# Loading the second MLP's weights earlier and with more room to land, and the keys of the first eight groups once

## The chip, the cores and the metric

One core of a Trainium2 chip runs the whole program. The metric is the time of one execution on the device in microseconds (us), and the figure quoted is the median of three executions. TensorE (PE) does the matrix products, VectorE (DVE), ScalarE (ACT) and GpSimd (POOL) the elementwise work, and SyncE (SP) issues nearly all DMA transfers. Each engine, and SP's queue of transfers too, runs its instructions in the order in which the program lists them: an instruction that waits holds up all that stand behind it on its engine.

## The reference

Three stages, each feeding the next, in float32 to the user (the weights arrive as float64):

```python
# q, k, v: 4 batches x 8 heads x 576 positions x 64
scores = scale * q @ k^T, masked to 0 <= row - column < 64
x = softmax(scores) @ v                  # 2304 tokens x 512
h = x @ w_in                             # 512 -> 2048
x = (h * sigmoid(1.702 * h)) @ w_out     # 2048 -> 512
xn = x / sqrt(mean(x * x) + 1e-6) * rms_g
out = (silu(xn @ w_gate) * (xn @ w_val)) @ w_out2   # 512 -> 1536 -> 512
```

## The kernel before

**Tiles.** The 2304 tokens are 36 attention groups of 64 tokens (nine per batch); each group attends to two neighbouring blocks of 64 keys. The first MLP takes the tokens in six blocks of 512, 256, 384, 384, 384 and 384. A block is 16 steps, one for each 128 of the 2048 hidden columns: an up product, the gate, and a down product two or more steps later. So there are 96 steps: 0 to 15 are the block of 512 ("block one"), 16 to 31 the block of 256 ("block two"), and from 32 on four blocks of 384. The second MLP follows in 36 units.

**Order.** No engine order is written by hand. Each operation is given to a planner (`Planner`, `pl.op`) with a cost for each engine that may run it, a priority `prio` (mostly the number of the step in which it is due; a smaller one goes first), what it reads and writes, and the tile buffers that it opens. `emit` plays the operations through in time: whenever an engine is free it takes, of those whose inputs are there and whose buffer is free, the one of least priority. What comes out is only an order for each engine and for SP's queue. A transfer counts there as done 2.2 us after its cost (bytes / 320 GB/s), and `late` adds to that: readers are put so much further down the order. On the chip the true waits are kept by semaphores. The tiles of a kind are taken in turn, and a tile is free when its last user is done.

**Second MLP's weights, first pass.** While the first MLP runs, the 36 weight pieces of the second are prepared (`b_narrow`, from line 1151): for each of 12 column chunks a gate, a value and an output piece. `w_narrow` (line 331) loads a piece of 512 KB into a tile of kind `raw` (line 336), and turns its float64 bits into float32: one ACT operation (line 340) and three of DVE (lines 344, 348, 354). The first MLP's 32 pieces went through the same three `raw` tiles in block one, the last of them loaded at 120.8 us. Two gate pieces (or two value pieces) make a pair: four sums and differences on DVE or POOL (line 1172) fill in their free halves, both tiles are stored to DRAM (`wp`, line 1175), and only when a store has landed is its `raw` tile free for another piece. Output pieces leave their `raw` tile for one of kind `y` and are stored from there (line 1158). Piece i has the place p = n0 + i * (n1 - n0) / 36 among the steps, with n0 = 34 and n1 = 76; it may be loaded once step int(p) - 2 has been run on PE, and its load has priority p, the work on it p + 3. Only output pieces have `late`, of 5 us. The first of these loads is issued at 194.8 us, the last at 423.8 us.

**Scatter at a block's end.** `a_finish` (from line 640) stores the block's result and the root mean squares: 1.5 KB go from a tile into DRAM one word at a time (`rs<-ss`, line 700), on SP's queue as well.

**Attention.** A group's chain is: scores on PE (line 428, in the first eight groups 432 and 435), mask and maximum on DVE, powers on ACT, normalization on POOL, transposition (on PE, or from group 18 on with DVE's 32 x 32 transpose, line 520, and copies of blocks by ACT and POOL, lines 312 and 314), values on PE (line 487). Keys, queries and values come in by lines 405, 398 and 413. The first eight groups run ahead of all else, from 4.5 to 31 us, with tiles of their own (`q0`, `k0`, `v0`): neighbouring groups share a block of keys, which each loads again.

Of the kernel before, what the change touches and what calls it, by code (L numbers as in the profile page):

```python
# [9 lines left out]
F32 = mybir.dt.float32  # L10
F32R = mybir.dt.float32r
I32 = mybir.dt.int32
# [5 lines left out]
P = 128  # L18
W = 64
# [182 lines left out]
def dma(nbytes):  # L202
    return max(nbytes / 320e3, 0.45)
# [3 lines left out]
def window_attention_two_moe_kernel(ctx: ExitStack, tc: tile.TileContext, ins, out):  # L207
    nc = tc.nc
    qh, kh, vh, w_in, w_out, w_gate, w_val, w_o2, rms_g = ins
    NBAT, NBLK = qh.shape[0], qh.shape[1]  # L210
    NT, DM = out.shape
    NK = DM // P
# [10 lines left out]
    NBA = len(sizes)  # L223
# [5 lines left out]
    NS = ngrp[0]  # L229
# [18 lines left out]
    ident = const.tile([P, P], F32, name="ident")  # L248
# [7 lines left out]
    start = sctx.enter_context(tc.tile_pool(name="start", bufs=1))  # L256
# [22 lines left out]
        "e": (at, 1, [P, NK, P], F32),  # L279
        "pt": (at, 1, [P, NK, P], F32),  # L280
        "t1": (at, 1, [P, NK, P], F32),
        "q0": (start, 4, [P, NK, 2 * W], F32),
        "k0": (start, 3, [P, 2, NK, W], F32),
        "v0": (start, 3, [P, DM], F32),
        "e0": (start, 4, [P, NK, P], F32),
        "pt0": (start, 1, [P, NK, P], F32),
# [9 lines left out]
    def make(b):  # L296
        if b.kind == "pt":
            b.tile = pts
            return pts
        if b.kind == "xa":  # L300
            turn = xa_turn[0] = 1 - xa_turn[0]
            b.tile = words(SUMS)[:, turn * 512:(turn + 1) * 512].rearrange("p (k c) -> p k c", k=NK)
            return b.tile
        p, n, shape, dt = KINDS[b.kind]
        b.tile = p.tile(shape, b.dt or dt, tag=b.kind, name=b.kind, bufs=n)
        return b.tile
# [19 lines left out]
    START = "start pool"  # L326
# [1 line left out]

    w32 = {}

    def w_narrow(key, src, prio, after=(), apart=False):
        rb = Buf("raw")
        fb = Buf("y") if apart else rb

        def fetch(e):
            nc.sync.dma_start(out=make(rb), in_=src.bitcast(I32).rearrange("p (n two) -> p n two", two=2))

        def scaled(e):
            high = rb.tile[:, :, 1].bitcast(F32)
            nc.scalar.activation(out=high, in_=high, func=AF.Copy, scale=2.0 ** -112)  # L340

        def shifted(e):
            low = rb.tile[:, :, 0]
            nc.vector.tensor_scalar(out=low, in0=low, scalar1=29, scalar2=None, op0=ALU.logical_shift_right)

        def joined(e):
            low, high = rb.tile[:, :, 0], rb.tile[:, :, 1]
            nc.vector.scalar_tensor_tensor(  # L348
                out=low, in0=high, scalar=3, in1=low, op0=ALU.logical_shift_left, op1=ALU.bitwise_or)

        def signed(e):
            low, high = rb.tile[:, :, 0], rb.tile[:, :, 1]
            to = make(fb).bitcast(I32) if apart else high
            nc.vector.scalar_tensor_tensor(
                out=to, in0=high, scalar=-2147483648, in1=low, op0=ALU.bitwise_and, op1=ALU.bitwise_or)

        got = pl.op({"D": dma(P * 4096)}, fetch, prio - 3, new=[rb], after=after, late=5.0 if apart else 0.0)
        pl.op({"A": act(512)}, scaled, prio, w=[rb])
        pl.op({"V": dve(512, True)}, shifted, prio, w=[(rb, "low")], after=[got], port="V")
        pl.op({"V": dve(512)}, joined, prio, w=[rb], r=[(rb, "low")], port="V")  # L360
        if apart:
            pl.op({"V": dve(512)}, signed, prio, r=[rb, "at"], new=[fb], port="V")
        else:
            pl.op({"V": dve(512)}, signed, prio, r=["at"], w=[rb], port="V")
        w32[key] = fb
# [25 lines left out]
    def wkey(g):  # L391
        b, i = divmod(g, NBLK)
        return b, max(i - 1, 0)
# [6 lines left out]
    def load_k(g, prio, kind="k"):  # L400
        if wkey(g) in kw:
            return
        b, i = wkey(g)
        t = kw[b, i] = Buf(kind)
        pl.op({"D": dma(P * 2048)}, lambda e: nc.sync.dma_start(out=make(t), in_=kh[b, :, i:i + 2]), prio, new=[t])

    def load_v(g, prio, kind="v"):
        if wkey(g) in vw:
            return
        b, i = wkey(g)  # L410
        t = vw[b, i] = Buf(kind)
        pl.op({"D": dma(P * 2048)},
              lambda e: nc.sync.dma_start(out=make(t), in_=vh[b, i * W:(i + 2) * W]), prio, new=[t])
# [4 lines left out]

    def attention(g, p0, step, ekind="e", ptkind="pt", norm=("G",), ptev=("A", "V"), hi=("A",)):
        q, k, v = q_of.pop(g), kw[wkey(g)], vw[wkey(g)]  # L420
        sb, eb, nb, ub, rb = Buf(f"y{g % 3}" if g < NS else "abank"), Buf(ekind), Buf("nm"), Buf("su"), Buf("rc")
        tb, pb, ob = Buf("bank" if g < NS else "abank"), Buf(ptkind), Buf("abank")
        extra = [START] if ekind == "e0" or ptkind == "pt0" or q.kind == "q0" or k.kind == "k0" or v.kind == "v0" else []

        def scores(e):
            s = make(sb)
            for p in range(NK):
                nc.tensor.matmul(s[:, p * P:(p + 1) * P], q.tile[:, p], k.tile[:, :, p], start=True, stop=True)  # L428

        def masked_scores(e):  # L430
            s = make(sb)
            nc.tensor.matmul(s.rearrange("p (k c) -> p k c", k=NK), ident_r,
                             (n_first if g % NBLK == 0 else n_rest).to_broadcast([P, NK, P]), start=True, stop=False)
            for p in range(NK):
                nc.tensor.matmul(s[:, p * P:(p + 1) * P], q.tile[:, p], k.tile[:, :, p], start=False,
                                 stop=(p == NK - 1))

        def highest_of(e):
# [59 lines left out]
        c = (g * W) % RING // W  # L498
        d = step
        if g < NS:  # L500
            pl.op({"T": 1.09}, masked_scores, p0, r=[q, k, "mask", "negative", "ident", *extra],
                  w=[("xh", c), ("xl", c), "scores order"], new=[sb])
            pl.op({"V": dve(512) + 0.1}, highest_of, p0, r=[sb], new=[nb])
            pl.op({"A": 4 * act(128, True, 2)}, powers_of, p0, r=[sb, nb, *extra], new=[ub, eb])
        else:
            pl.op({"T": 0.872}, scores, p0, r=[q, k, *extra], w=[("xh", c), ("xl", c), "scores order"], new=[sb, eb],
                  after=vals[NS - 1:NS] if g >= NS else ())
            pl.op({"V": dve(512)}, masked, p0, r=[sb, "mask"], w=[eb])
            pl.op({"V": dve(512)}, highest, p0, r=[eb], new=[nb])
            pl.op({"A": 4 * act(128, True, 2)}, powers, p0, r=[nb], w=[eb], new=[ub])  # L510
# [234 lines left out]
    def both(n, alone=False):  # L745
        return {"V": dve(n)} if alone else {"G": pool(n), "V": dve(n)}
# [336 lines left out]
    for g in range(NS):  # L1083
        late = g >= 2
        load_q(g, -90 + 2 * g, "q0" if late else "q")
        load_k(g, -89 + 2 * g, "k0" if g > 2 else "k")
        load_v(g, -84 + 2 * g, "v0" if g > 2 else "v")
    for g in range(NS):
        attention(g, -60 + g, 0.5, "e0" if g >= 2 else ("e", "t1")[g], "pt0" if g % 2 else "pt",
# [48 lines left out]
        b_list.append((("v", c), w_val[c], c - c % 2 + 1))  # L1138
        b_list.append((("o", c), w_o2[c], c + 2))
    b_list.sort(key=lambda x: x[2])  # L1140
    n0, n1 = first[2] + 2, first[NBA - 1] - 4

    def ex_open(e):
        actx.close()
# [6 lines left out]
    def b_narrow(i):  # L1151
        (kind, c), src, _ = b_list[i]
        p = n0 + i * (n1 - n0) / len(b_list)
        key = ("w32d", "o", c) if kind == "o" else ("w32d", c - c % 2 + "gv".index(kind), c % 2)
        w_narrow(key, src, p + 3, after=[ups[int(p) - 2]], apart=kind == "o")
        b = w32.pop(key)
        if kind == "o":
            pl.op({"D": dma(P * 2048)}, lambda e: nc.sync.dma_start(out=w32o_d[c], in_=b.tile), p + 3, r=[b], w=[key])
            return
        n = key[1]  # L1160
        if c % 2 == 0:
            halfway[n] = b
            return
        pair = (halfway.pop(n), b)

        def word(h, k, lane):
            return pair[h].tile[:, k * 256:(k + 1) * 256, lane].bitcast(F32)

        for to, x, y, op in (((0, 0), (1, 0, 1), (1, 1, 1), ALU.add), ((0, 1), (0, 0, 0), (0, 0, 1), ALU.subtract),
                             ((1, 0), (0, 0, 1), (1, 0, 1), ALU.subtract), ((1, 1), (0, 1, 1), (0, 1, 0), ALU.subtract)):  # L1170
            xs = [(n, "sum", *v[:2]) for v in (x, y) if v[2] == 0]
            fn = lambda e, to=to, x=x, y=y, op=op: eng[e].tensor_tensor(out=word(*to, 0), in0=word(*x), in1=word(*y), op=op)
            pl.op(both(256), fn, p + 3, r=[*pair, *xs], w=[(n, "sum", *to)], port="GV")
        for h in range(2):
            pl.op({"D": dma(P * 4096)}, lambda e, h=h: nc.sync.dma_start(
                out=w32p_d[n][:, h].bitcast(I32), in_=pair[h].tile), p + 3,
                r=[pair[h], (n, "sum", h, 0), (n, "sum", h, 1)], w=[("w32d", n, h)])

    plans.sort()
# [97 lines left out]
```

## Time and profile before

| | us |
|---|---|
| median of three runs | 937.48 (937.11 to 937.95) |
| the profiled execution, whole | 937.76 |
| its span, first to last instruction | 936.0 |
| PE busy | 909.0 |
| DVE busy | 648.8 |
| ACT busy | 436.4 |
| POOL busy | 275.3 |

| stretch of the span, us | what PE does there |
|---|---|
| 4.5 to 33 | scores, transposes and values of the first eight groups |
| 33 to 128 | block one (512 tokens), with four groups |
| 128 to 193 | block two (256 tokens), with six groups |
| 193 to 504 | blocks three to six, with 18 groups |
| after | the second MLP |

The profile lists each engine's instructions with start and length, and for an engine that stood idle what ended its wait. A time such as "us, times, longest" adds up such waits. PEclk is the share of full clock that TensorE was granted; it has two levels, 1.0 (2.4 GHz) and 0.5 (1.2 GHz), and a value between them is a mean over the stretch.

### The profile page before, as it was taken

The numbers are of one execution on the slowest core, as the hardware profiler recorded it, in microseconds if no ns is written. First come the engines' busy times: TensorE is split into PE (matmuls) and PEld (weight loads), VectorE is DVE, ScalarE is ACT, GpSimd is POOL, SyncE is SP. The second block draws the span as 40 slices with busy tenths as digits, with TensorE's granted clock in tenths as the row PEclk, the third lists the DMA queues.
The fourth block names the chain that finished last, engine by engine and source line by source line (L and its number), as shares of the span: only waits on it lengthen the run. The fifth ranks groups of instructions, "written<-read, shape, count | busy, mean of one in ns | idle before, by whom it ended". The sixth has DMA issues, their size and how long they took to land.

```text
span 936.0 us, 15370 instructions
## 1 busy us (share of the span) xinstructions
PE 909.0 (97%) x5436; PEld 843.1 (90%) x5436; DVE 648.8 (69%) x1237; ACT 436.4 (47%) x1078; POOL 275.3 (29%) x389
## 2 busy tenths in 40 slices
PE   8899999998999999999999999999999999999998
PEld 7787789988899999989999889998999999999997
DVE  5999974465777677675367888878767556555553
ACT  6666664464566567456336534454322224322222
POOL 4111021132345345333012633334223225222210
PEclk9899999999899999999999999999999999999999
DMA  8756532348666566753565999977987677976651
GB/s 274 237 182 203 175 121 56 109 139 192 224 220 205 180 228 240 184 205 122 68 236 172 302 280 332 369 277 246 319 247 209 204 204 235 291 204 205 203 153 67
DMA packets 86536, 194.63 MB, mean 208 GB/s; under 512 B 12726, under 2 KB 36027, under 8 KB 84924
## 3 DMA queue, kind: packets, MB, share of 16 engines
q1 hardware_dynamic: 66108, 137.02, 45.4%
q0 software_dynamic: 20352, 56.63, 20.5%
q8 instruction: 43, 0.70, 0.3%
q14 instruction: 33, 0.27, 0.1%
HBM read 140.13 MB, written 53.50 MB: 207 GB/s over the span
## 4 chain that ended last, share of the span: by engine, by line
PE 69%; DVE 13%; DMA 9%; issue 3%; ACT 3%; POOL 1%; SPq 1%; DVEq 0%; ACTq 0%; POOLq 0%
PE bank L912 8%; PE bank L913 8%; PE bank L914 8%; PE y L628 4%; PE y L630 4%; PE y L629 4%; PE bank L555 4%; PE bank L554 4%; PE bank L556 4%; PE y L1013 3%; PE y L1015 3%; PE y L1014 3%; DMA wp<-raw 3%; DVE raw L348 3%; PE abank L428 2%
## 5 line engine op out<-in xcount | busy, mean ns | idle before, releaser
L554 PE MATMUL bank<-xh,slab 128*128 128x384 f32 (+2 forms) x288 | 99.6, 346 | 0.8 <-DVE th L611 0.8
L556 PE MATMUL bank<-xh,slab 128*128 128x384 f32 (+2 forms) x288 | 97.5, 339 | 1.9 <-DVE slab L381 1.9
L628 PE MATMUL y<-gh,slab 128*128 128x384 f32 (+2 forms) x288 | 98.4, 342 | 0.0
L555 PE MATMUL bank<-xl,slab 128*128 128x384 f32 (+2 forms) x288 | 97.7, 339 | 0.5 <-DVE xl L494 0.5
L630 PE MATMUL y<-gh,slab 128*128 128x384 f32 (+2 forms) x288 | 96.9, 336 | 0.0
L629 PE MATMUL y<-gl,slab 128*128 128x384 f32 (+2 forms) x288 | 96.9, 336 | 0.0
L951 ACT ACTIVATE sb<-gh 128x384 f32<-128x384 f32 x72 | 37.8, 525 | 113.6 <-DVE gh L938 113.5
L312 ACT ACTIVATE xh<-sb 128x384 fp32r<-128x384 f32 x72 | 37.1, 521 | 105.9 <-DVE sb L966 105.9
L938 DVE TENSOR_TENSOR gh<-gl,bank 128x384 f32<-128x384 f32 x108 | 59.3, 551 | 37.3 <-PE bank L914 36.8
L611 DVE SCALAR_TENSOR_TENSOR th<-th,bank 128x384 f32<-128x384 f32 (+2 forms) x96 | 52.6, 547 | 44.9 <-ACT th L607 44.8
L913 PE MATMUL bank<-slab,late 128*128 128x384 f32 x228 | 77.1, 338 | 0.0
L913 PE MATMUL bank<-slab,slab 128*128 128x384 f32 x228 | 76.5, 335 | 0.0
L607 ACT ACTIVATE th<-bank 128x384 f32<-128x384 f32 (+2 forms) x96 | 46.4, 483 | 59.1 <-PE bank L556 53.4
L472 POOL TENSOR_TENSOR e<-e,rc 128x512 f32<-128x512 f32 x34 | 37.0, 1087 | 121.4 <-DVE rc L469 97.5
L312 ACT ACTIVATE gh<-th 128x384 fp32r<-128x384 f32 (+2 forms) x96 | 50.2, 524 | 43.6 <-DVE th L611 40.2
L938 DVE TENSOR_TENSOR gl<-gl,bank 128x384 f32<-128x384 f32 x72 | 39.8, 553 | 35.7 <-PE bank L914 32.1
L340 ACT ACTIVATE raw<-raw 128x512 f32<-128x512 f32 x68 | 46.1, 682 | 29.3 <-DMA raw<-in_w_gate_dram 11.0
L569 DVE TENSOR_TENSOR gl<-th,gh 128x384 fp32r<-128x384 f32 (+2 forms) x74 | 44.5, 601 | 21.1 <-ACT gh L312 20.6
L556 PEld LDWEIGHTS bank<-xh,slab 128*128 128x128 f32 x288 | 54.5, 189 | 4.8 <-DVE slab L381 2.7
L463 ACT ACTIVATE e<-e,nm 128x128 f32<-128x128 f32 x112 | 43.6, 391 | 32.0 <-DVE nm L458 31.9
L554 PEld LDWEIGHTS bank<-xh,slab 128*128 128x128 f32 x288 | 54.7, 190 | 3.7 <-DVE th L611 1.8
L555 PEld LDWEIGHTS bank<-xl,slab 128*128 128x128 f32 x288 | 54.7, 190 | 2.9 <-DVE xl L494 0.9
(197 smaller groups left out, 2631.2 us busy)
## 6 DMA issues: line engine op xcount, KB each, us to landing
slab<-wc POOLq DMA_DIRECT2D x36, 512.0 KB, 4.8
late<-wc POOLq DMA_DIRECT2D x36, 512.0 KB, 4.2
wp<-raw SPq DMA_DIRECT2D x24, 512.0 KB, 2.7
fw<-wp SPq DMA_DIRECT2D x12, 1024.0 KB, 11.4
late<-wo POOLq DMA_DIRECT2D x22, 512.0 KB, 5.5
q<-in_q_dram SPq DMA_DIRECT2D x36, 256.0 KB, 4.8
wc<-slab SPq DMA_DIRECT2D x18, 512.0 KB, 7.3
wc<-late SPq DMA_DIRECT2D x18, 512.0 KB, 6.1
```

The lines of the kernel that those rows point to most:

```text
L312: nc.scalar.activation(out=out, in_=in_, func=AF.Copy)
L554: nc.tensor.matmul(h, w[:, 0, kk], xh_ring[:, kk, cols], start=(kk == 0), stop=False)
L555: nc.tensor.matmul(h, w[:, 0, kk], xl_ring[:, kk, cols], start=False, stop=False)
L556: nc.tensor.matmul(h, w[:, 1, kk], xh_ring[:, kk, cols], start=False, stop=(kk == NK - 1))
L611: nc.vector.scalar_tensor_tensor(out=th, in0=th, scalar=1.0, in1=hb.tile[:, 0:n], op0=ALU.add, op1=ALU.mult)
L628: nc.tensor.matmul(y, s[:, 0, cols], hb.tile[:, 0:n], start=first, stop=False)
L629: nc.tensor.matmul(y, s[:, 0, cols], lb.tile[:, 0:n], start=False, stop=False)
L630: nc.tensor.matmul(y, s[:, 1, cols], hb.tile[:, 0:n], start=False, stop=last)
L912: nc.tensor.matmul(h, w[:, 0, kk], xh[:, kk], start=kk == 0, stop=False)
L913: nc.tensor.matmul(h, w[:, 0, kk], xl[:, kk], start=False, stop=False)
L914: nc.tensor.matmul(h, w[:, 1, kk], xh[:, kk], start=False, stop=kk == 1)
L938: nc.vector.tensor_tensor(out=(make(to) if kind else s.tile)[:, 0:HT].bitcast(F32), in0=s.tile[:, 0:HT].bitcast(F32), in1=b.tile[:, 0:HT], ...
```

## The change

Two edits that don't depend on each other.

One: the pieces of the second MLP start 18 steps earlier (n0 is step 16, the first of block two, and no longer 34), end where they did, and so stand 60 / 36 = 1.67 steps apart, no longer 42 / 36 = 1.17. Their load gets `late` = 6 us for all kinds, and priority p + 5; the work on them, sums and stores have p + 8. The condition on step int(p) - 2 stays as it is written.

Two: the keys of the first eight groups lie in one tile `kall` of eight blocks, and each block is loaded once, by a transfer of 128 KB; before, seven transfers of 256 KB brought two blocks each. To make room there are three `q0` tiles, no longer four.

```diff
-        "q0": (start, 4, [P, NK, 2 * W], F32),
-        "k0": (start, 3, [P, 2, NK, W], F32),
+        "q0": (start, 3, [P, NK, 2 * W], F32),
+        "kall": (start, 1, [P, NS, NK, W], F32),
...
-    def w_narrow(key, src, prio, after=(), apart=False):
+    def w_narrow(key, src, prio, after=(), apart=False, late=0.0):
...
-        got = pl.op({"D": dma(P * 4096)}, fetch, prio - 3, new=[rb], after=after, late=5.0 if apart else 0.0)
+        got = pl.op({"D": dma(P * 4096)}, fetch, prio - 3, new=[rb], after=after, late=late)
...
+    def load_k_once(g, prio):
+        b, i = wkey(g)
+        kw[b, i] = (kall, i)
+        for n in (i, i + 1):
+            if n not in kseen:
+                def load(e, n=n):
+                    if kall.tile is None:
+                        make(kall)
+                    nc.sync.dma_start(out=kall.tile[:, n], in_=kh[b, :, n])
+
+                kw_ = {"w": [(kall, n)], "hold": [kall]} if kseen else {"new": [kall], "w": [(kall, n)]}
+                kseen.add(n)
+                pl.op({"D": dma(P * 1024)}, load, prio, **kw_)
...
-        load_k(g, -89 + 2 * g, "k0" if g > 2 else "k")
+        load_k_once(g, -89 + 2 * g)
...
-    n0, n1 = first[2] + 2, first[NBA - 1] - 4
+    n0, n1 = first[1], first[NBA - 1] - 4
...
-        w_narrow(key, src, p + 3, after=[ups[int(p) - 2]], apart=kind == "o")
+        w_narrow(key, src, p + 8, after=[ups[int(p) - 2]], apart=kind == "o", late=6.0)
...
-            pl.op(both(256), fn, p + 3, r=[*pair, *xs], w=[(n, "sum", *to)], port="GV")
+            pl.op(both(256), fn, p + 8, r=[*pair, *xs], w=[(n, "sum", *to)], port="GV")
...
-                out=w32p_d[n][:, h].bitcast(I32), in_=pair[h].tile), p + 3,
+                out=w32p_d[n][:, h].bitcast(I32), in_=pair[h].tile), p + 8,
```

The scores of the first eight groups read `kall.tile[:, i:i + 2]` in place of a tile of their own.

## Rows read from the trace of the kernel before

**Rows 1.** The page's part 1: busy us, share of the span, instructions, by engine.
```profile
PE 909.0 (97%) x5436; PEld 843.1 (90%) x5436; DVE 648.8 (69%) x1237; ACT 436.4 (47%) x1078; POOL 275.3 (29%) x389
```

**Rows 2.** PE's waits: waiting and releasing work, us in total, times, longest.
```profile
PE abank L487 <- POOL pts L314: 7.1, 5, 4.0
...
PE y L435 <- DMA k<-in_k_dram: 0.2, 1, 0.2
```

**Rows 3.** Busy us and instructions by stretch (PE, PEld, DVE, ACT, POOL), PEclk, DMA.
```profile
228.00:236.00 8.00, 3.82 (x22) 3.34 (x20) 5.72 (x13) 5.01 (x18) 5.05 (x9) 0.93 0.72 252
236.00:244.00 8.00, 7.48 (x43) 7.37 (x44) 7.12 (x12) 4.86 (x15) 2.26 (x3) 0.64 0.68 238
...
390.00:398.00 8.00, 7.22 (x41) 6.90 (x41) 3.62 (x8) 3.91 (x13) 0.95 (x1) 1.00 0.79 231
398.00:406.00 8.00, 6.12 (x40) 5.58 (x40) 6.44 (x13) 4.77 (x13) 4.58 (x8) 0.79 0.54 198
```

**Rows 4.** Chain of waits, 376 to 406 us: start, length, what.
```profile
381.89 9.99 DMA wp<-raw
...
391.89 4.18 DMA raw<-in_w_gate_dram
...
402.90 2.01 PE abank L428 x8
```

**Rows 5.** SP's queue in order of time, 196 to 240 us: start, length, line, transfer.
```profile
209.22 0.39 SPq L700 DMA_DIRECT2D rs<-ss  x1
...
210.21 0.86 SPq L1175 DMA_DIRECT2D wp<-raw  x2
221.28 0.33 SPq L336 DMA_DIRECT2D raw<-in_w_val_dram  x1
```

**Rows 6.** ACT and DVE in order of time, 203 to 238 us; in brackets the wait before.
```profile
224.92 0.68 ACT L340 ACTIVATE raw<-raw 128x512 f32<-128x512 f32 x1 [6.43 <-DMA raw<-in_w_val_dram]
...
224.91 0.43 DVE L344 TENSOR_SCALAR raw<-raw 128x512 int32<-128x512 int32 x1 [5.83 <-DMA raw<-in_w_val_dram]
```

**Rows 7.** Waits of SP's queue: us in total, times, longest.
```profile
SPq L336 <- DMA wp<-raw: 43.5, 17, 10.1
```

**Rows 8.** Transfers: line 700 by itself, then KB each and median us to landing.
```profile
L700 SPq DMA_DIRECT2D rs<-ss x6: 370/377/388, 152.2 to 535.6; - x6
...
DMA to landing us min/median/max: 9.6/9.6/9.6
...
wp<-raw SPq DMA_DIRECT2D x24, 512.0 KB, 2.7
...
raw<-in_w_in_dram SPq DMA_DIRECT2D x16, 512.0 KB, 3.5
```

**Rows 9.** As Rows 3: block two, and block one after its first steps.
```profile
128.00:193.00 65.00, 63.47 (x575) 60.65 (x574) 31.16 (x69) 33.67 (x107) 13.04 (x14) 1.00 0.31 90
...
40.00:125.00 85.00, 83.01 (x427) 66.56 (x426) 82.32 (x147) 55.57 (x113) 9.18 (x7) 1.00 0.56 190
```

**Rows 10.** DVE's groups of work on raw tiles, 194 to 440 us: busy us, mean ns.
```profile
L348 DVE SCALAR_TENSOR_TENSOR raw<-raw 128x512 int32<-128x512 int32 x36 | 30.0, 834 | 3.5 <-ACT raw L340 3.0
...
L354 DVE SCALAR_TENSOR_TENSOR raw<-raw 128x512 int32<-128x512 int32 x24 | 17.8, 741 | 0.3
L344 DVE TENSOR_SCALAR raw<-raw 128x512 int32<-128x512 int32 x36 | 16.1, 448 | 14.7 <-DMA raw<-in_w_gate_dram 8.8 <-DMA raw<-in_w_val_dram 5.8
...
L1172 DVE TENSOR_TENSOR raw<-raw 128x256 f32<-128x256 f32 x30 | 12.4, 444 | 0.1
```

**Rows 11.** The start: stretch of 5 us as Rows 3; a wait of ACT.
```profile
5.00:10.00 5.00, 4.16 (x27) 3.57 (x25) 2.33 (x5) 2.31 (x7) 0.00 (x0) 1.00 1.04 361
...
ACT e L448 <- DVE nm L442: 1.5, 1, 1.5
```

**Rows 12.** The start in order of time: SP's query of group six, PE's scores of group five.
```profile
9.39 0.33 SPq L398 DMA_DIRECT2D q<-in_q_dram  x1
...
15.20 1.05 PE L435 MATMUL y<-k,q 128*128 128x128 f32 x8
```

More of the change, by code (lines that the diff above doesn't have):

```diff
@@ L405, in load_k @@
         pl.op({"D": dma(P * 2048)}, lambda e: nc.sync.dma_start(out=make(t), in_=kh[b, :, i:i + 2]), prio, new=[t])
+    kall = Buf("kall")
+    kseen = set()
+    def load_k_once(g, prio):
[10 more added lines that the diff above has]
+                pl.op({"D": dma(P * 1024)}, load, prio, **kw_)
     def load_v(g, prio, kind="v"):
@@ L420, in attention, with keys @@
         q, k, v = q_of.pop(g), kw[wkey(g)], vw[wkey(g)]
+        kt = [k]
+        if isinstance(k, tuple):
+            kt = [(kall, k[1]), (kall, k[1] + 1)]
+        def keys():
+            return kall.tile[:, k[1]:k[1] + 2] if isinstance(k, tuple) else k.tile
+        held = [kall] if isinstance(k, tuple) else []
         sb, eb, nb, ub, rb = Buf(f"y{g % 3}" if g < NS else "abank"), Buf(ekind), Buf("nm"), Buf("su"), Buf("rc")
         tb, pb, ob = Buf("bank" if g < NS else "abank"), Buf(ptkind), Buf("abank")
-        extra = [START] if ekind == "e0" or ptkind == "pt0" or q.kind == "q0" or k.kind == "k0" or v.kind == "v0" else []
+        extra = [START] if ekind == "e0" or ptkind == "pt0" or q.kind == "q0" or isinstance(k, tuple) or v.kind == "v0" else []
         def scores(e):
@@ L427, in scores @@
             for p in range(NK):
-                nc.tensor.matmul(s[:, p * P:(p + 1) * P], q.tile[:, p], k.tile[:, :, p], start=True, stop=True)
+                nc.tensor.matmul(s[:, p * P:(p + 1) * P], q.tile[:, p], keys()[:, :, p], start=True, stop=True)
         def masked_scores(e):
@@ L434, in masked_scores @@
             for p in range(NK):
-                nc.tensor.matmul(s[:, p * P:(p + 1) * P], q.tile[:, p], k.tile[:, :, p], start=False,
+                nc.tensor.matmul(s[:, p * P:(p + 1) * P], q.tile[:, p], keys()[:, :, p], start=False,
                                  stop=(p == NK - 1))
@@ L500, in attention @@
         if g < NS:
-            pl.op({"T": 1.09}, masked_scores, p0, r=[q, k, "mask", "negative", "ident", *extra],
+            pl.op({"T": 1.09}, masked_scores, p0, r=[q, *kt, "mask", "negative", "ident", *extra], hold=held,
                   w=[("xh", c), ("xl", c), "scores order"], new=[sb])
@@ L505, in attention @@
         else:
-            pl.op({"T": 0.872}, scores, p0, r=[q, k, *extra], w=[("xh", c), ("xl", c), "scores order"], new=[sb, eb],
+            pl.op({"T": 0.872}, scores, p0, r=[q, *kt, *extra], hold=held, w=[("xh", c), ("xl", c), "scores order"], new=[sb, eb],
                   after=vals[NS - 1:NS] if g >= NS else ())
@@ L1154, in b_narrow @@
         key = ("w32d", "o", c) if kind == "o" else ("w32d", c - c % 2 + "gv".index(kind), c % 2)
-        w_narrow(key, src, p + 3, after=[ups[int(p) - 2]], apart=kind == "o")
+        w_narrow(key, src, p + 8, after=[ups[int(p) - 2]], apart=kind == "o", late=6.0)
         b = w32.pop(key)
         if kind == "o":
-            pl.op({"D": dma(P * 2048)}, lambda e: nc.sync.dma_start(out=w32o_d[c], in_=b.tile), p + 3, r=[b], w=[key])
+            pl.op({"D": dma(P * 2048)}, lambda e: nc.sync.dma_start(out=w32o_d[c], in_=b.tile), p + 8, r=[b], w=[key])
             return
```

## The prediction
> **What bounds the kernel now.** I read the page first: PE is busy for 909.0 of 936.0 us [rows 1], so nothing but PE's idle time, and the time that it spends at the low clock, can be won: 27 us and a little more. The second view is the list of PE's waits. Its largest entry is the values product (line 487) waiting for POOL's copies of the transposed powers, 7.1 us in five waits, one of 4.0 us [rows 2]. POOL is hardly the cause, at 29% busy; what holds it up has to be looked for. So the third view is a table of short stretches. Two of them stand out [rows 3]: around 235 us PE is idle for 8.00 - 3.82 = 4.18 us, then for 0.52, and after that idle time the granted clock falls to a mean of 0.64 for 8 us; around 400 us it is idle for 0.78 + 1.88 us, with a clock of 0.79.
>
> Who is late there, the chain of waits and SP's queue tell. At 209.2 us SP issues the word-wise store of block two's mean squares (a scatter of 4-byte pieces), which takes 9.6 us to land, though it is small [rows 5, 8]. The two stores of a finished pair stand right behind it (210.2 us). Such a store lands after a median of 2.7 us [rows 8], here only after some 10 [rows 4]. Until then its `raw` tile is not free, and SP waits with the next load: 43.5 us over 17 waits, the longest 10.1 [rows 7]. The load goes out at 221.28 [rows 5] and lands 3.5 us later, as these loads do [rows 8]. ACT and DVE have the work on that piece next in their order and stand still for 6.43 and 5.83 us [rows 6]. All behind it, gates and the chain of one attention group, shifts by as much; PE works off what it had in hand, and stops at that group's values. So the two long stalls are one thing: a slow store, a tile that is free late, and two in-order engines that wait for a landing which the order had put 3.8 us after the issue.
>
> **The change part by part.**
>
> *More time to land.* The order now counts a load as landed after 1.6 + 2.2 + 6 = 9.8 us, no longer 3.8. At 235 us the store took 11 us where the order counts 3.8, and the load 3.6: 14.6 us against 7.6 planned before and 13.6 planned now. So 7 us of lateness become 1 us, and ACT's wait of 6.43 us goes down to about that; the second case has 10.0 + 4.2 = 14.2 us [rows 4], so 0.6 remains. What the two stalls cost, by [rows 3]: the first 4.18 + 0.52 idle, and (1 - 0.64) x 8 = 2.9 us of full-speed work lost to the clock (up to 0.6 more in the stretch before); the second 0.78 + 1.88 idle and (1 - 0.79) x 8 = 1.7. That is 7.6 to 8.1 and 4.3 us, 12 in all. Taken as -12. Next in line is the attention chain itself, which met its steps in the other blocks.
>
> The clock is part of this price only because PE stood still: the rows show eight scores products taking 2.01 us just behind the second stall [rows 4], and a clock of 1.00 wherever PE has no gap [rows 9].
>
> *Earlier start, wider spacing.* The work itself is the same. A piece costs DVE 834 + 741 + 448 ns and 30/36 of a sum at 444: 2.4 us [rows 10]. Block two has room: DVE is busy for 31.2 of its 65 us [rows 9]. Three `raw` tiles limit how many pieces pass there. With 9.8 us to land, then two or three for the work, the sums, and 3.8 for the store, a pair and an output piece need some 20 us, so about eight pieces fit: 19 us more, DVE 77% busy. In block one DVE is 97% busy and PE idle for 1.99 of 85 us, while block two, with DVE half idle, has 1.53 of 65 [rows 9]: a busy DVE alone costs PE little. Bounds: -1.5 (all that idle time goes) and +4.3 (one stall as at 400 us). Taken: +1.5, the rate of block one added once more, since steps of 256 tokens leave an attention chain less time. After 193 us DVE loses those 19 us; I count nothing for that.
>
> *Loads moved past other entries of SP's queue.* Eight loads and some stores now go out in block two, among its attention loads. The scatter at 152.2 us, the first of six [rows 8], had no raw transfer near it; now it may have. A load issued right behind a scatter lands after 9.6 + 3.5 = 13.1 us, 3.3 later than the order counts. ACT's wait of 6.43 us cost PE 8, so about 1 us for 1. The first four scatters lie in the stretch of the raw loads, each with some chance of it. Bounds 0 and 4 x 3.3 = 13; taken +1.5, half a case.
>
> *Stores and lower priority.* p + 8 lets gates and attention go ahead of this work where both are ready. Its last piece may load after the same step, 72, as before, and is due at step 82; the tiles of the second MLP are first wanted at step 84. Nothing, unless the pieces fall behind by more than two steps.
>
> *Keys once.* 7 x 256 KB become 8 x 128 KB, 768 KB fewer; at the 361 GB/s of the busiest stretch [rows 11] 2.2 us of transfer time. Of it PE feels 0.2 us, its whole wait for keys [rows 2]. From 9 us on the start hangs on ACT's 32 powers, whose one gap is 1.5 us [rows 11]. Against that group zero now needs two key transfers, one SP issue later. With three `q0` tiles the query of group five waits for group two's scores, as that of group six did (9.39 us), and is wanted at 15.20 [rows 12]: 5.8 us later, enough by 2 us for a lone transfer, barely in a full queue. Bounds -1.5 and +1; taken 0.
>
> A rule speaks against this part. The Trainium skill, "SBUF — State Buffer", section "The DMA setup-cost knee", gives every transfer a fixed 2 us beside its bytes at 436 GB/s. By that, my estimate from the page, seven loads of 256 KB one after another take 18.2 us and eight of 128 KB 18.4: nothing gained. The stretch at 361 GB/s [rows 11], with transfers of 256 KB and less, is not one in which they run singly, so I hold with the bytes. It changes nothing in the sum.
>
> **Sum.** -12 + 1.5 + 1.5 + 0 = -9.0. The profiled execution took 937.76 us, 1.8 more than its span and 0.3 more than the median of 937.48; from the median, 928.5.
>
> **The rivals.**
> - *Half of it* (0.21): one raw load per block or two comes to lie right behind a scatter, at 3.3 to 6.6 us in all on top of the sum. For it: the scatter is untouched, and loads are now spread over more block ends. Against: a load takes one of many places in the queue. 931.8 to 935, as a point 933.5.
> - *It doesn't do what it says* (0.12): the order puts the work on a piece at the first idle moment after the counted landing; where engines were full it stood later than that anyway, and the added 6 us move little; or a store behind the scatter then holds three tiles and the lateness grows with it. The stalls move and stay: 937, 935.6 to 939.4. For it: 17 waits of SP for a store [rows 7], most of which cost nothing. Against: ACT stood still for the landing itself [rows 6].
> - *Slower* (0.15): tiles live 6 us longer, so that from block two on the three of them are emptied together and refilled by three loads in a row. Where a scatter stands in front, all three land 4 us or more late, and every block end gets a stall at the price of the second one, 4.3 us: 4 x 4.3 = 17.2, less the 12 that go, + 5: 942.5. It decides the sign from the third such stall on (3 x 4.3 = 12.9). For it: the cycle of 20 us for three pieces is just about the spacing in block two. Against: from block three on, pieces come 1.67 steps of some 5 us apart, 25 us for three.
>
> **How the numbers follow.** The forecast has 0.52, with a range of its own of 922.5 to 933 (the bounds of keys and of block two, and 2 us of small waits). About 0.2%, 1.9 us, is what a measurement here can tell from no change. Faster: forecast and half of it, 0.73. Same: 0.12. Slower: 0.15. A range of 922.5 to 938 leaves out the slower case and a little below.
>
> **What would show it.** Right: ACT's and DVE's waits for raw loads fall from 6 us to 1 or 2 at the longest, PE's wait for POOL's copies falls from 7.1 to under 2, the granted clock is 1.00 from 40 us to 500, DVE is some 75% busy in block two, and the first scores start at 4.5 us as before. Wrong: a new wait over 3 us of ACT for a raw load just after a scatter, a PE gap between 128 and 193 us of more than 3 us, or a start that is longer by a microsecond. If SP's waits for stores grow beyond 43.5 us and PE's idle time does too, it was the slower case.

## The result, and the profile after

The changed kernel takes 928.76 us (median of four; 927.58 to 930.39), the kernel before 937.72 in the same runs: a ratio of 0.990, with a 95% interval from 0.9873 to 0.9926. The forecast was 928.5.

The page of the changed kernel: its span, busy time by engine, and the granted clock in 40 slices.

```profile
span 927.7 us, 15378 instructions
PE 905.1 (98%) x5436; PEld 839.6 (91%) x5436; DVE 646.1 (70%) x1231; ACT 439.2 (47%) x1081; POOL 279.7 (30%) x392
PEclk9899999999999999999999999999999999999999
```

PE does the same 5436 products in a span that is 8.3 us shorter. The slice with a lower clock around 235 us is gone; the one from 23 to 46 us stands.

PE's waits, as in [rows 2]:

```profile
PE abank L512 <- ACT pts L312: 1.9, 3, 1.0
PE bank L937 <- DVE gl L963: 1.8, 2, 1.2
...
PE abank L512 <- DVE raw L344: 1.4, 1, 1.4
...
PE y L460 <- DMA kall<-in_k_dram: 0.4, 1, 0.4
```

The 7.1 us for POOL's copies, the largest entry before, are not in the list any more, and no single wait reaches 2 us.

Busy time by stretch, as in [rows 3, 9]: the start of block one, the rest of it, block two, blocks three and after.

```profile
33.00:40.00 7.00, 7.00 (x23) 5.62 (x23) 4.37 (x9) 4.50 (x13) 2.86 (x3) 0.66 0.65 230
40.00:125.00 85.00, 82.12 (x417) 65.32 (x416) 78.83 (x138) 52.93 (x108) 13.23 (x10) 0.98 0.52 175
128.00:193.00 65.00, 63.44 (x548) 59.85 (x547) 45.78 (x92) 35.38 (x102) 17.30 (x18) 1.00 0.65 184
193.00:440.00 247.00, 245.30 (x1681) 237.97 (x1680) 165.32 (x321) 155.61 (x458) 99.98 (x165) 1.00 0.51 174
```

The first and the last of these stretches in the kernel before:

```profile
33.00:40.00 7.00, 6.98 (x32) 5.47 (x32) 6.38 (x13) 5.12 (x15) 2.06 (x2) 0.96 0.58 177
...
193.00:440.00 247.00, 238.49 (x1586) 230.53 (x1586) 175.19 (x338) 147.47 (x435) 99.76 (x166) 0.98 0.63 198
```

From 193 us on PE idles for 1.7 us where it idled for 8.5, at full clock. DVE's share in block two went from 31.2 to 45.8 us of 65. In block one the changed kernel is worse: from 33 to 40 us PE runs at a mean clock of 0.66 and does 23 products, where it did 32 at 0.96, and DVE, busy for 97% of 40 to 125 us before, is busy for 93%.

Where the time went shows best in the start of each step's first up product on PE, taken from the two traces (us):

| step | before | after | difference |
|---|---|---|---|
| 0 (block one) | 33.0 | 33.2 | +0.2 |
| 8 | 76.8 | 82.4 | +5.6 |
| 16 (block two) | 128.0 | 132.9 | +4.9 |
| 32 (block three) | 193.6 | 200.2 | +6.6 |
| 40 | 227.0 | 234.4 | +7.4 |
| 44 | 254.6 | 254.5 | -0.1 |
| 72 | 392.3 | 389.4 | -2.9 |
| 76 | 417.2 | 409.6 | -7.6 |
| 95 | 499.6 | 489.7 | -9.9 |

The changed kernel loses 6.6 us by the end of block two, and its last row lies 16.5 us better than that. The two long stalls lie in the steps 40 to 44 and 72 to 76: 7.5 and 4.7 us. The last row flatters it: when step 95 begins, the changed kernel has one down product more left to do than the kernel before (12 matrix products, 2.1 us). At the last down product of the first MLP, which starts at 515.8 us before and at 507.9 in the changed kernel, the difference is 7.9 us, so some 14.5 us are gained after block two. Behind that it stays so (8.3 us at the end of the span).

What PE gained there came with another order in SP's queue. In the kernel before, two of the three scatters with a pair's stores behind them have these at a distance of 1.0 and 1.9 us (209.22 and 210.21, 378.83 and 380.74). In the changed kernel the distances are 8.0, 5.2 and 7.2 us. Scatter and stores at the end of block two and of block four, and what SP's loads still wait for stores [rows 7]:

```profile
214.99 0.38 SPq L725 DMA_DIRECT2D rs<-ss  x1
222.95 1.85 SPq L1200 DMA_DIRECT2D wp<-raw  x2
...
375.01 0.38 SPq L725 DMA_DIRECT2D rs<-ss  x1
...
382.21 1.59 SPq L1200 DMA_DIRECT2D wp<-raw  x2
...
SPq L336 <- DMA wp<-raw: 18.0, 11, 4.8
```

These waits were 43.5 us, the longest 10.1.

### The profile page after: what moved, and what is told of

Its sections match the earlier page's. It is cut to its first block, busy times and chain, and to the rows that moved or that the text cites. A ratio compares the mean times of both kernels' runs of the same rounds, so it can differ in the third digit from the quotient of the medians.

```text
span 927.7 us, 15378 instructions
## 1 busy us (share of the span) xinstructions
PE 905.1 (98%) x5436; PEld 839.6 (91%) x5436; DVE 646.1 (70%) x1231; ACT 439.2 (47%) x1081; POOL 279.7 (30%) x392
## 4 chain that ended last, share of the span: by engine, by line
PE 79%; DVE 10%; DMA 6%; ACT 2%; issue 2%; SPq 0%; POOL 0%; ACTq 0%; DVEq 0%; POOLq 0%
PE bank L937 8%; PE bank L938 8%; PE bank L939 8%; PE bank L579 6%; PE bank L581 6%; PE bank L580 6%; PE y L655 6%; PE y L653 6%; PE y L654 6%; PE y L1038 3%; PE y L1040 3%; PE y L1039 3%; PE abank L453 3%; PE abank L512 2%; PE abank L1038 2%
## 5 line engine op out<-in xcount | busy, mean ns | idle before, releaser
L655 PEld LDWEIGHTS y<-gh,slab 128*128 128x128 f32 x288 | 54.5, 189 | 4.2 <-DVE slab L381 2.1
L653 PEld LDWEIGHTS y<-gh,slab 128*128 128x128 f32 x288 | 54.4, 189 | 3.2 <-DVE y L678 0.7
```

What stands on the lines that cost most here:

```text
L653: nc.tensor.matmul(y, s[:, 0, cols], hb.tile[:, 0:n], start=first, stop=False)
L655: nc.tensor.matmul(y, s[:, 1, cols], hb.tile[:, 0:n], start=False, stop=last)
```

## The experiments

**Which part does it.** Four kernels, each the kernel before with a part of the change. A ratio is to the kernel before, run alongside, with its 95% interval.

*Keys alone.* The first eight groups' keys as in the change, three `q0` tiles; `b_narrow` as before.

> Only the keys of the first eight groups are loaded once (with three q0 tiles); the raw loads stay as before. If the later PE of the changed kernel in block one (step 8 began at 82.4 us, before at 76.8) comes from the keys, step 8 begins near 82 us here too, both long stalls stay and the time is 940 to 943 us. If it comes from the raw loads' new places, step 8 begins near 77 us and the time is 937 to 938.

939.36 us, a ratio of 1.0029 (1.0009 to 1.0049), in neither expected range: the keys cost some 2.7 us, by the interval 0.8 to 4.6. The trace doesn't show where. Step 8 begins at 78.9 us, 2.1 late, step 16 at 129.3, and step 95 at 500.7, 1.1 late. But in the traces of the twelve kernels with the old keys, the one before among them, step 16 begins anywhere between 127.2 and 130.8 us, so one trace can't place 1 or 2 us. Only the full change, at 132.9, lies outside.

*Raw loads alone.* Sums and stores get p + 8 as well.

```diff
-    n0, n1 = first[2] + 2, first[NBA - 1] - 4
+    n0, n1 = first[1], first[NBA - 1] - 4
...
-        w_narrow(key, src, p + 3, after=[ups[int(p) - 2]], apart=kind == "o")
+        w_narrow(key, src, p + 8, after=[ups[int(p) - 2]], apart=kind == "o", late=6.0)
```

> Only the raw loads are changed (earlier start, 6 us more to land, priority p + 8); keys as before. If the loss in block one comes from the keys, the start and block one are as before (step 16 at 128 us) and the time is 923 to 925 us, better than the full change. If it comes from the raw loads' new places, 927 to 930.

927.41 us, 0.9892 (0.986 to 0.9924). This part is the whole gain, as far as the runs can tell: its total and that of the full change can't be told apart. Step 16 begins at 129.8 us, within the spread of the kernels with the old keys.

*More time to land, without the earlier start* (`n0` as before, the rest of the raw loads' part):

> The raw loads get 6 us more to land and priority p + 8, but begin at step 34 as before, 1.17 steps apart; keys as before. Theory (the margin takes up the lateness of stores behind a scatter): no stall over 1.5 us after 193 us, 926 to 930 us. Rival (what helped is that pieces stand wider apart): three tiles, held 6 us longer, fall behind with 1.17 steps a piece, stalls stay, 934 to 940.

952.79 us, 1.0164 (1.0142 to 1.0186). Both expectations missed it, the theory's by far. Two stretches of this kernel, columns as in [rows 3]:

```profile
193.00:340.00 147.00, 146.27 (x999) 142.36 (x996) 96.37 (x191) 87.93 (x260) 59.76 (x105) 0.99 0.51 166
340.00:450.00 110.00, 98.50 (x620) 94.63 (x620) 74.33 (x142) 59.81 (x174) 32.66 (x54) 0.92 0.54 177
```

Up to 340 us PE idles for 0.7 us and the stall at 235 us is gone. Here too, though, the pair's stores are issued 6.6 us behind block two's scatter (216.12 and 209.49). Then the work piles up. The loads of output pieces, first and last issue in this kernel (the second line is the kernel before):

```profile
L336 SPq DMA_DIRECT2D raw<-in_w_o_dram x12: 327/330/1093, 223.7 to 470.6; - x12
...
L336 SPq DMA_DIRECT2D raw<-in_w_o_dram x12: 327/377/752, 222.1 to 423.8; - x12
```

The last load comes 47 us later, its work meets the ends of blocks, and the second MLP's first preparation waits: the loads of its root mean squares begin at 485.0 us, before at 449.6. At 680 us there is a further stall of 7 us, in which DVE waits 8.2 us for such a load; why that one is late wasn't followed. The likely reason for the pile is that three tiles, each held longer, can't take a piece every 1.17 steps. By the prediction's working a pair and an output piece need some 20 us, and three places 1.17 steps apart, at 4.8 us a step (134.9 us for the steps 44 to 72 of the changed kernel), give 17: some 37 us lost over 12 such rounds, an estimate, of the 47. This kernel has the lower priority too, and no run has the margin without it at the old spacing. So margin and priority together need the earlier start, as the rival said; that it is for the tiles' sake is argued.

*Earlier start without the margin* (`n0` = step 16, everything else as before):

> The pieces begin at step 16 and stand 1.67 steps apart, but load and work keep their old margin (5 us for output pieces alone, priority p + 3); keys as before. Theory: stores behind scatters still make ACT and DVE wait 3 to 6 us for a raw load, in block two as well, so 934 to 938 us. Rival (spacing): no such waits, 926 to 930.

951.14 us, 1.0145 (1.0118 to 1.0172): the theory's side, and far worse than its number. Block two now has the stall that block three had. DVE, PE in order of time, and the longest waits of ACT:

```profile
170.81 0.43 DVE L344 TENSOR_SCALAR raw<-raw 128x512 int32<-128x512 int32 x1 [7.60 <-DMA raw<-in_w_gate_dram]
...
172.80 1.12 PE L477 MATMUL abank<-ident,e 128*128 128x128 f32 x4 [6.32 <-POOL e L472]
...
ACT raw L340 <- DMA raw<-in_w_gate_dram: 14.1, 2, 7.9
ACT raw L340 <- DMA raw<-in_w_val_dram: 11.9, 4, 8.2
```

The scatter goes out at 155.25 us, the pair's stores from 155.92 on, the next load at 164.26, and DVE waits until 170.81: the chain of [rows 4 to 6] once more, a block earlier.

**Margin or priority.** Two kernels with the earlier start, each with one of the two other edits. The first has `late=6.0` and p + 3:

> Earlier start and 6 us more to land, with the old priority p + 3. If the margin is what makes the earlier start bearable, 926 to 931 us, as with p + 8. If the lower priority does it, 938 to 951.

930.71 us, 0.9931 (0.9911 to 0.9952). The second has p + 8 and `late` as before:

> Earlier start and priority p + 8, with the old margin to land (5 us for output pieces alone). If the margin is what counts, the stalls of the earlier start alone stay: 943 to 951 us. If the lower priority counts, 926 to 932.

941.23 us, 1.0043 (1.0025 to 1.0061), between its two expectations. With the earlier start, the margin takes 951 to 931, the priority alone 951 to 941, both 927. The margin is the larger part, and the priority without it is more than the nothing that I had put down. What the priority adds to the margin (931 to 927) isn't clear of noise, for the intervals overlap.

The first of the two shows the margin at work: a raw load is issued 3.9 us behind block two's scatter there (216.19 and 212.28). DVE waits 3.0 us for that piece, and PE no more than 0.9 us at once between 205 and 250 us.

**What makes the store late.** In the kernel before, the scatter (line 700) sent from POOL's queue:

```diff
-            nc.sync.dma_start(out=rs_d[j].rearrange("one (t p) -> p (one t)", p=P), in_=cb.tile[:, 0:n // P])
+            nc.gpsimd.dma_start(out=rs_d[j].rearrange("one (t p) -> p (one t)", p=P), in_=cb.tile[:, 0:n // P])
```

> The kernel before with one edit: the word-wise store of the mean squares at a block's end goes out on POOL's queue, no longer on SP's. If that store standing ahead of the pair's stores in one queue makes the long stalls, those land within 4 us, the stalls at 235 and 400 us go and the time is 925 to 929 us. If they were slow for another reason (transfer engines busy, not the queue), the stalls stay: 935 to 938.

941.45 us, 1.004 (1.0007 to 1.0074). POOL and SP in order of time:

```profile
210.28 0.78 POOL L700 DMA_DIRECT2D rs<-ss  x1
...
210.81 1.82 SPq L1175 DMA_DIRECT2D wp<-raw  x2
221.08 0.33 SPq L336 DMA_DIRECT2D raw<-in_w_val_dram  x1
```

The load that waits for the first store still goes out 10.3 us after it (before: 11.1 [rows 5]). So the delay doesn't need the same queue. The Trainium skill, "DMA: Bandwidth & Descriptors", section "Issuing engines are not separate DMA queues", says that transfers of all issuing engines run on the same 16 DMA engines and interleave; this trace agrees, with 10 us on either queue. The total is a poor measure of that, for POOL's waits for the gather before it grew from 17.0 to 33.0 us.

The same edit on the earlier start alone:

> The earlier start with the old margin and priority (951 us), and the word-wise store on POOL's queue. If the store is what made block two stall, DVE's wait of 7.6 us for a raw load near 171 us goes, and so do most of the 14 us: 930 to 938. If block two is simply too full, 945 to 952.

945.7 us, 1.0086 (1.0062 to 1.011): 5 us better than without it, at the lower end of the second expected range. Block two keeps its stall (step 32 begins at 205.4 us, 11.8 late). Where the 5 us come from wasn't followed.

Next, the pieces. Reading and storing the root mean squares with neighbouring words per partition leaves the result as it is, since what is done to them is done word by word:

```diff
-            nc.sync.dma_start(out=make(cb)[:, 0:n // P], in_=ms_d[j].rearrange("one (t p) -> p (one t)", p=P))
+            nc.sync.dma_start(out=make(cb)[:, 0:n // P], in_=ms_d[j].rearrange("one (p t) -> p (one t)", p=P))
...
-            nc.sync.dma_start(out=rs_d[j].rearrange("one (t p) -> p (one t)", p=P), in_=cb.tile[:, 0:n // P])
+            nc.sync.dma_start(out=rs_d[j].rearrange("one (p t) -> p (one t)", p=P), in_=cb.tile[:, 0:n // P])
```

> The kernel before with one edit: the root mean squares of a block are read and stored with 2 to 4 neighbouring words per partition, where before each word was a piece by itself, so the store has 128 pieces, no longer 256 to 512. If the number of pieces is what keeps the store, and whatever comes after it, for 10 us, the stores of pairs behind it land within 5 us, the stalls near 235 and 400 us shrink to under 2 us and the time is 926 to 931 us. If it is not, 936 to 940.

923.24 us, 0.9843 (0.981 to 0.9875): by 5 us better than the change, with intervals that just touch, and with no load moved. Line 700, its landing, SP's queue, the waits for stores, the longest waits for raw loads of the second MLP, and a stretch:

```profile
L700 SPq DMA_DIRECT2D rs<-ss x6: 320/326/384, 154.6 to 523.2; - x6
...
DMA to landing us min/median/max: 2.5/3.9/4.2
...
211.53 0.38 SPq L700 DMA_DIRECT2D rs<-ss  x1
...
212.48 0.86 SPq L1175 DMA_DIRECT2D wp<-raw  x2
218.38 0.33 SPq L336 DMA_DIRECT2D raw<-in_w_val_dram  x1
...
SPq L336 <- DMA wp<-raw: 30.8, 17, 5.0
...
ACT raw L340 <- DMA raw<-in_w_gate_dram: 2.9, 5, 1.1
ACT raw L340 <- DMA raw<-in_w_val_dram: 2.8, 3, 1.3
...
193.00:440.00 247.00, 245.73 (x1673) 238.68 (x1674) 180.31 (x352) 156.35 (x452) 99.48 (x166) 1.00 0.60 202
```

The store lands in 3.9 us, no longer 9.6. The order of the transfers is that of [rows 5], the store again behind the scatter, and the load goes out 5.9 us after it, no longer 11.1. ACT's waits for gate and value pieces fall from 18.9 us to 5.7, with none above 1.3, and PE is as free after 193 us as in the changed kernel. Both long stalls are gone: the steps 40 to 44 take 20.1 us, before 27.6, and the steps 72 to 76 take 20.0, before 24.9. The Trainium skill, "DMA: Bandwidth & Descriptors", section "Rules for kernel authors", says that a transfer whose last dimension isn't contiguous becomes one descriptor for each element. The packets under 512 bytes agree: 12726 in the kernel before, 9654 here, 3072 fewer, which is 2 x 2304 words less 2 x 6 x 128 pieces.

That the store's form makes the stalls is shown; that it is the number of pieces is not, for with fewer pieces each is longer, and neighbouring words no longer come from different partitions. The number alone fits badly. Word by word a store has as many pieces as its block has tokens. Block two's 256 landed after 9.6 us before and 8.8 in the changed kernel; the four landings recorded with the scatter on POOL's queue, three of them of 384 pieces, took 8.2 to 11.4. The gather isn't it: it goes out at 204.31 us before, lands within 4 us, and the store is issued at 209.22 [rows 5].

*The same edit with the earlier start alone:*

> The earlier start with old margin and priority (951 us), with 2 to 4 neighbouring words per partition in the store at a block's end. If that store is what makes the earlier start slow, its 14 us go, and with them the stalls of the kernel before: 926 to 934. If the earlier start is slow by itself, 943 to 951.

926.7 us, 0.9865 (0.9828 to 0.9902). The 14 us that the earlier start had cost are gone: they hung on the form of the store.

*The same edit with the raw loads' part of the change:*

> The raw loads' part of the change (927.4 us) and 2 to 4 neighbouring words per partition in the store at a block's end. If the 6 us already hide what the store costs, nothing more is gained: 925 to 929. If lateness remains that they don't hide (the stalls of 1 to 2 us in block two), 921 to 925.

924.34 us, 0.9845 (0.9817 to 0.9872). That is 3 us better than the raw loads' part by itself, which the intervals don't quite separate, and no better than the edit alone: with a store that lands early, margin, priority and earlier start bring nothing that these runs can tell.

**The keys' cost.** The kernel before with three `q0` tiles, nothing else:

> The kernel before with three tiles q0 in place of four; keys, raw loads and all else as before. If the keys' part of the change costs its 1 to 3 us because a query waits for a tile, 938 to 940.5 us. If it costs them because group zero's keys come in two transfers, or because the order of block one falls out another way, 936 to 938.

937.92 us, 0.9997 (0.9975 to 1.002). The missing query tile by itself shows no cost, though up to 1.9 us isn't excluded. Group zero's keys in two transfers, or the order of block one, remain; they were not told apart.

## Why the prediction was right, and where it wasn't

- *What bounds the kernel*: right. That the two long stalls are one thing, a slow store near the pair's stores, was argued from the order of three rows [rows 5]; the edit of the store's form shows it for both. That a transfer is late because it *stands behind the scatter in SP's queue*, so that 9.6 and 3.5 us add up, is not: the scatter on another queue delays the stores as much.
- *More time to land* (-12): right in size. The two stalls gave 7.5 + 4.7 = 12.2 us in the table of steps. But the mechanism was right in part only. By my working 14.6 us of lateness stay and the margin covers 13.6 of them. In the changed kernel most of that lateness doesn't arise: the pair's stores go out 5 to 8 us behind the scatters, no longer 1 to 2 as at the two long stalls, and SP's waits for stores fall from 43.5 to 18.0 us. I hadn't counted with another order; which of the edits makes it was not told apart. That the margin does cover a late load is shown by the kernel with earlier start and margin alone, and by the load of 11.8 us below. And margin and lower priority at the old spacing gave +15 us. The limit of three tiles was in the working, and used for block two only, not for pieces at the old spacing.
- *After 193 us* "I count nothing": there the full change won some 2 us more than the two stalls (14.5 less 12.2), most of it between the steps 44 and 72, which took 2.7 us less (1.1 of it PE's idle time).
- *Earlier start* (+1.5): block two became 1.7 us longer (+4.9 at step 16, +6.6 at step 32), with the term that follows included; DVE was 70% busy there where 77% was forecast.
- *Loads moved past a scatter* (+1.5): a load right behind a scatter happened once, much as described. Chain of waits and DVE's release, 150 to 172 us, in the changed kernel:

```profile
156.45 0.38 SPq L725
...
156.88 11.77 DMA raw<-in_w_o_dram
...
168.67 0.43 DVE raw L344
...
170.71 0.69 PE abank L512 x16
```

  The load took 11.8 us, 2 more than the order counts where 3.3 were forecast, and PE's wait at 170.71 was 0.8 us: less than the 3.3 us of the rival *half of it*. Stores behind the other scatters cost nothing that PE shows.
- *Stores and lower priority*: put at nothing; with the earlier start it is worth 10 us without the margin (951 to 941). What it is worth with the margin (931 to 927) is not clear of noise.
- *Keys once* (0, from -1.5 to +1): wrong. They cost 2.7 us (0.8 to 4.6) by the runs of that part alone; the bytes saved, with which the prediction held, brought nothing that shows. The full change has 4.9 us of lateness by step 16. The first scores wait for a key transfer until 5.67 us; that is 0.6 of it. The rest lies in block one and isn't settled; step 16 differs by 3.6 us among the kernels with the old keys, so a part of it may be no more than that. The clock of 0.66 up to 40 us isn't a mark of the keys: the kernel with the keys alone has 1.00 in that stretch.

So the sum of -9.0 came out right by terms that were off either way: 4.9 us lost by step 16 that I hadn't counted, against some 2 us won after block two that I hadn't counted and 1.3 us less lost in block two than the 3.0 put down. Between the two traces the span fell by 8.3 us, and by the medians the time fell by 9.0; that these meet the forecast within 0.3 us is luck. The likeliest case was the one that came; none of the rivals did. The rival *slower* named the three tiles as what decides, and the kernel with margin and priority at the old spacing, 15 us slower, speaks for it.

## What to carry to other kernels

When in-order engines stand still for a load, follow the chain to the transfer that was late first, and ask what it shared with its neighbours: here a store of 1 to 2 KB, written word by word, held up 512 KB transfers beside it for 10 us, and giving it neighbouring words brought at least as much as moving 36 loads around it. A margin for landing costs buffer time; here it paid where pieces came no faster than the held buffers came free. And when consumers are moved, look whether the transfers moved too: the order that came out had taken the stores away from the scatter. A term that is put at nothing because it lies off the path (a priority, a reordered start) wants bounds as wide as those of the terms that are counted.

## What the runs showed of the hardware that was not expected

A word-wise store of 256 pieces of 4 bytes (block two's; the 1.5 KB of the part on the kernel before are those of a block of 384) lands after 9.6 us. Two 512 KB stores issued within 2 us of it land only after some 10 us, where the median is 2.7, with the scatter on SP's queue or on POOL's. With 128 pieces of two to four words it lands after 3.9 us (2.5 to 4.2), and the load behind those stores can go out after 5.9 us. The gather of single words (`ss<-ms`) landed in a median of 3.7 us before and 3.6 with the longer pieces: it is the store that gains by them, not the gather.
